# A fused chunk-selecting attention and gated FFN on one core: two more units and one more block turned by crossbar transposes, row copies issued as transfers

## The chip, the cores and the metric

The kernel runs on one core of one Trainium2 chip. The metric is device time in microseconds (us) of one launch. Where a launch was also profiled, its own time and the span that the profiler saw are given beside each other. Engines are named as in the profile: PE (matrix products, PEld its weight loads), DVE (vector), ACT (scalar), POOL (GpSimd) and SP (the engine that issues most transfers).

## What is computed

There are 4 batches of 8 heads, 768 rows and a head size of 64. Keys are cut into 24 chunks of 32 rows. For each query and chunk an upper bound of the scores is made from the chunk's smallest and largest key per dimension; the 6 chunks with the highest bound are kept, and a causal softmax attention runs over these alone. The result, 3072 rows of 512, goes through a gated FFN of width 1536.

```
k_min, k_max = min / max of each 32-row chunk of k
ub   = sum_d max(q * k_min, q * k_max);  ub[chunk after the row's own] = -1e9
sel  = the 6 chunks with the largest ub
attn = softmax(where(sel and causal, q k^T / 8, -1e9))
x    = (attn @ v) laid out as [3072, 512]
out  = (sigmoid(x @ w_gate) * (x @ w_val)) @ w_out
```

## The kernel before, in words

The 24 blocks of 128 rows (4 batches of 6) are dealt to eight units of three blocks. Unit 0 holds the first blocks of batches 0 to 2, whose rows need no selection. Unit 1 is blocks 1 to 3 of batch 0; unit 2 is blocks 4 and 5 of batch 0 and, as a third column, the first block of batch 3; unit 3 is blocks 1 to 3 of batch 1; units 4 to 7 go on through batches 1 to 3.

For each unit the work goes through the same stages. Keys are turned and reduced to chunk extremes (`keys_wide` for batch 0, `keys_blocks` for the others), and copied by rows into the key store `hk` (ops named `hk…`, line 741). Queries are turned (`turn_queries`), and `choose` makes the bounds on PE, the six largest on DVE, and mask rows, which are copied under the queries (ops `hqm…`, line 825). `attend` (line 832) does scores on PE, exponentials on ACT, the causal cut on POOL, products with the values on PE. `finish` (line 895) divides on DVE and turns the result of two heads into `xT`, so that features lie on partitions. For units 1 to 3 that turn is one PE transpose for each block (line 914), into a PSUM bank, and one copy out of it (line 918, run by the helper `copy`, lines 353 and 355); from unit 4 on (`u.i >= XBAR`, with `XBAR = 4`) it is one crossbar transfer issued by SP (line 905). `first` (line 590) does the unselected blocks: it turns keys and queries in float32 on PE (line 600), copies them out as float16 (line 604), and turns its result on PE too (line 666). Units 0 to 3 each have an FFN of their own (`ffn`: 48 gate products, 48 value products and so on, line 937, then `project_out`, line 968); units 4 and 5, and 6 and 7, share a form that needs 7 products in place of 8 (`ffn_pair`, line 1054, `project_pair`, line 1195), whose input sums (ops `S…`, line 1177) go to DVE or POOL and whose evictions (ops `E…`, `F…`) go to ACT or DVE.

What sets the order is a string, `ORDER`. It holds the 1964 operations in one list; each engine runs its own in the order of the list and waits only for the data and buffers that it needs. A word may name an engine (`hk0_u2_1@ACT`) and the buffer slots that the op takes first (`:5,2`). Without a name the first engine of the op's list is taken. The numbers in the code such as `dve(S)` or `dma=(1200, 256)` are costs that were used in making the list; they do not act at run time. SP's list is in order too: a transfer whose data is not there yet holds back those behind it.

Of the kernel before, what the change touches and what calls it, by code (L numbers as in the profile page):

```python
# [119 lines left out]
g_u0_11:1,0,11 kx1_u2_3 cm_u1_0 sc_u1_0_1:4 kt_u2_3@DVE:0 v_u0_11:7 hkf1 exp_u1_0_1 kx0_u2_3 tanh_u0_9 v16_0_3  # L120
o0_u0_0:4,0 kt_u2_0:2 hg_u0_9 tanh_u0_11 hk1_u2_3@POOL hk1_u2_0 kt_u2_1:1 sc_u1_1_1:5 q2_u2 o1_u0_0 hg_u0_11
hk0_u2_1@ACT q3_u2 kx0_u2_1 exp_u1_1_1 k11_1:0 hq1_u1_0 qf1_3:2 v16_0_2 o2_u0_0 v16_0_1 hk0_u2_3@POOL pv_u1_2:6
osb_u0_0@DVE kfT_3:3 qn_u2_3:4 sc_u1_5_0:2,2 kcr_u2 qn_u2_2:2 pv_u1_1:1 kf16_3@DVE:0 qf0_3 pv_u1_0 qT_u2_3:7 out_u0_0
rz_u1_0:0 qT_u2_2:0 sc_u1_6_2:5,3 pv_u1_3 k01_1 qf_u2_2 sc_u1_7_0:4,0 exp_u1_5_0 rz_u1_1:1 o0_u0_1:3,1 vf_3:1 qm_u2_2
qf_u2_3@DVE hq0_u2_2 x_u1_0:0 exp_u1_6_2 sc_u1_7_2:0 sc_u1_4_2:2,1 x_u1_1:2 exp_u1_7_2 sc_u1_7_1:7 o1_u0_1 exp_u1_4_2
qm_u2_3 exp_u1_7_0 qm_u2_0 sc_u1_5_2:1 hq1_u2_1 sc_u1_6_0:5 cm_u1_7 exp_u1_7_1 sc_u1_5_1:0 cm_u1_5 exp_u1_5_1
sc_u1_4_0:6 ub_u2:2,4 k10_1 exp_u1_6_0 k00_1 exp_u1_5_2 xps_u1_0:7,1 exp_u1_4_0 sc_u1_6_1:0 ubn0_u2:0 sc_u1_4_1:5
qfT_3:1 xT_u1_0 exp_u1_4_1 cm_u1_4 mx0_u2:0 o2_u0_1 hk0_u2_0@ACT hq0_u2_3@POOL ubn1_u2 exp_u1_6_1 hq1_u2_3@POOL
pv_u1_5:2 qf16_3:6 mx1_u2 cm_u1_6 pv_u1_7:6 vc_3@ACT pv_u1_4 v_0_5:5 hq1_u2_0@DVE pv_u1_6 rz_u1_2:0 scf_3:7,5,0 ap1_u2
o0_u0_2:4,0 apt1_u2:0 expf_3_0 ap0_u2 expf_3_1:2 rz_u1_3:1 x_u1_2:1 o1_u0_2 cmf_3_0 hqm1_u2_0@ACT apt0_u2 cmf_3_1  # L130
x_u1_3:0 v_0_4:3 xps_u1_1:0 hq1_u2_2 sc_u2_4_2:1,1 xps_u1_2:7 hqm0_u2_2@DVE osb_u0_1 pvf_3_0:5 xps_u1_3:2 o2_u0_2
xT_u1_1@ACT xT_u1_3 out_u0_1 xT_u1_2 hqm1_u2_2@DVE sc_u2_3_0:6,3 v_1_1:4 kx0_1_3 pvf_3_1:3 sc_u2_7_2:2,0 exp_u2_3_0
sc_u2_3_2:0 q00_1:1 g_u1_0:7,3,12 exp_u2_3_2 rzf_3_1:0 cm_u2_3 xf_3_1:2 osb_u0_2 v_u1_0:6 q01_1 hqm0_u2_0 rzf_3_0:0
xf_3_0:1 tanh_u1_0 sc_u2_3_1:0 v16_0_5 kx1_1_1:0 exp_u2_7_2 g_u1_1:3,1,13 exp_u2_3_1 v16_0_4 v_u1_1:4 kx1_1_0
exp_u2_4_2 k16_1_3:3 tanh_u1_1 xpsf_3_0:5,0 xpsf_3_1:7 sc_u2_1_1:2,2 hg_u1_1 sc_u2_1_2:0 k16_1_0:5 g_u1_2:1,2,14
exp_u2_1_2 kx1_1_3 exp_u2_1_1 pv_u2_3:3 k16_1_1:4 q10_1 sc_u2_7_1:4 xTf_3_0@ACT kx1_1_2 sc_u2_1_0:0 tanh_u1_2 v_u1_2:2
exp_u2_1_0 sc_u2_0_0:5,3 hg_u1_2 g_u1_3:1,0,15 cm_u2_1 k16_1_2:2 hg_u1_0 sc_u2_0_2:0 v_u1_3:2 v_1_3:0 tanh_u1_3
kx0_1_2 xTf_3_1@ACT g_u1_4:6,1,16 exp_u2_7_1 hg_u1_3 sc_u2_0_1:1 kt_1_0:0 tanh_u1_4 pv_u2_1:7 v_u1_4:4 exp_u2_0_0
q11_1 sc_u2_2_1:2,2 cm_u2_0 hg_u1_4 g_u1_5:6,2,17 exp_u2_2_1 kx0_1_1 sc_u2_2_0:5 exp_u2_0_1 v_u1_5:4 tanh_u1_5 kx0_1_0
sc_u2_7_0:2 exp_u2_0_2 sc_u2_4_0:1 g_u1_6:6,3,0 hg_u1_5 k11_2:0 v_u1_6:0 kt_1_1:6 tanh_u1_6 v_1_0:2 exp_u2_7_0 pv_u2_0  # L140
kt_1_3:1 sc_u2_2_2:4 g_u1_7:6,0,2 exp_u2_2_2 exp_u2_2_0 hg_u1_6 sc_u2_4_1:2 v_u1_7:4 tanh_u1_7 qf0_u3_2:0 cm_u2_2
exp_u2_4_0 g_u1_8:5,1,1 kt_1_2:3 v16_1_3 out_u0_2 pv_u2_2 hk1_u2_1@POOL k10_2 tanh_u1_8 qf0_u4_0:1 sc_u2_6_1:0,3
kcr_1@POOL sc_u2_6_0:6 rz_u2_1:0 v16_1_1 k00_2 exp_u2_6_1 v_u1_8:1 x_u2_1:0 qf0_u3_0 cm_u2_7 exp_u2_6_0 g_u1_9:5,2,4
hk1_1_1 qf0_u3_1 exp_u2_4_1 v_u1_9:3 qm_u3_0:0 cm_u2_6 sc_u2_6_2:0 qf0_u4_1 sc_u2_5_0:6,2 rz_u2_0:0 exp_u2_6_2 hg_u1_7
g_u1_10:2,3,3 tanh_u1_9 qf0_u3_3 v_u1_10:0 v_1_4:1 tanh_u1_10 hg_u1_9 qm_u3_2@POOL exp_u2_5_0 sc_u2_5_2:4
g_u1_11:5,0,5 hg_u1_10 hk1_1_0@ACT x_u2_0:1 v_u1_11:2 hg_u1_8 cm_u2_5 hq0_u3_2@ACT ub_u3:3,6 cm_u2_4 v_2_1:5
hq0_u3_0@POOL tanh_u1_11 v_1_2:3 hk1_1_3@ACT hg_u1_11 v16_1_0 o0_u1_0:0,1 ubn1_u3:0 hq1_u3_0@ACT hk0_1_1 qf0_u4_2
k01_2 xps_u2_0:7 o1_u1_0 ubn0_u3 hk0_1_0 hk0_1_3@ACT ubm1_u3 mx1_u3:0 o2_u1_0 exp_u2_5_2 ubm0_u3 ap1_u3 xT_u2_0@ACT
hq1_u3_2 o0_u1_1:1,0 osb_u1_0 qf0_u4_3 mx0_u3 sc_u2_5_1:5 out_u1_0 o1_u1_1 exp_u2_5_1 ap0_u3 hk0_1_2@ACT apt1_u3:0
q10_2:1 pv_u2_5:2 apt0_u3 pv_u2_6:6 q00_2 pv_u2_4 hqm1_u3_2@ACT hqm0_u3_0@DVE hqm0_u3_2 o2_u1_1 kx1_2_2:1 hk1_1_2  # L150
sc_u3_0_0:3,3 sc_u3_0_1:4 xps_u2_1:7 exp_u3_0_0 sc_u3_0_2:0 sc_u3_1_0:5,1 rz_u2_2:0 hqm1_u3_0 pv_u2_7 x_u2_2:2
osb_u1_1 o0_u1_2:3,1 kx1_2_1 q11_2 xT_u2_1@ACT cm_u3_0 exp_u3_0_1 sc_u3_1_1:2 exp_u3_1_0 rz_u2_3:0 kx0_2_1
sc_u3_3_0:1,0 exp_u3_0_2 sc_u3_6_1:7,2 o1_u1_2 cm_u3_1 exp_u3_1_1 x_u2_3:1 k16_2_3@ACT:5 v16_1_2 kx0_2_0 sc_u3_1_2:4
out_u1_1 k16_2_0:4 exp_u3_1_2 sc_u3_3_2:5 o2_u1_2 k16_2_1@ACT:1 kx1_2_0 xps_u2_3:0 xps_u2_2:4 xT_u2_2 xT_u2_3@ACT
q01_2 sc_u3_6_0:6 exp_u3_6_0 pv_u3_0:2 pv_u3_1 sc_u3_7_0:0,3 exp_u3_7_0 exp_u3_6_1 kt_2_3:3 kx1_2_3 kt_2_0:5 rz_u3_0:0
g_u2_0:4,0,1 tanh_u2_0 v_u2_0:6 v_3_0:3 sc_u3_2_0:7,1 g_u2_1:0,1,3 hg_u2_0 kx0_2_2 exp_u3_3_0 cm_u3_3 cm_u3_7 cm_u3_6
v_u2_1:1 exp_u3_3_2 k16_2_2:4 osb_u1_2 v_2_2:2 out_u1_2 sc_u3_3_1:5 exp_u3_3_1 g_u2_2:3,3,4 v_u2_2:6 exp_u3_2_0
cm_u3_2 sc_u3_2_1:7 exp_u3_2_1 g_u2_3:5,0,5 v_u2_3:4 g_u2_4:7,2,0 x_u3_0:2 qf0_u6_3:0 qf1_u4_2 kx0_2_3 qf1_u4_3
qf1_u4_1 tanh_u2_1 sc_u3_6_2:0 sc_u3_2_2:2 tanh_u2_3 hg_u2_3 qf1_u4_0 tanh_u2_2 hg_u2_2 hg_u2_1 v_u2_4:3 g_u2_5:4,0,2
hk0_2_3 tanh_u2_4 pv_u3_3:1 exp_u3_2_2 pv_u3_2 kt_2_1:0 rz_u3_1:0 qm_u4_0@ACT:0 v_u2_5:2 tanh_u2_5 hg_u2_5 hg_u2_4  # L160
sc_u3_5_0:4,1 exp_u3_5_0 x_u3_1:1 hq0_u4_2@ACT qf0_u6_2 sc_u3_7_1:6 exp_u3_7_1 v16_2_1 qm_u4_2@POOL v_3_4:4 k10_3:0
v_2_3:5 qf0_u6_1 k11_3 kcr_2@POOL ub_u4:7,5 ubn0_u4:0 ubm0_u4 sc_u3_4_2:1,0 exp_u3_6_2 sc_u3_4_0:3 exp_u3_4_0 hk0_2_0
sc_u3_5_2:4 exp_u3_5_2 g_u2_6:6,2,16 tanh_u2_6 xps_u3_1:7,1 xT_u3_1@ACT kt_2_2:1 v_u2_6:3 g_u2_7:6,0,17 tanh_u2_7
v_u2_7:7 g_u2_8:4,1,12 sc_u3_7_2:6 v_u2_8:0 sc_u3_5_1:2 ubn1_u4 ubm1_u4 mx1_u4:0 hq0_u4_0@POOL exp_u3_4_2 hk0_2_2@ACT
hq1_u4_0@POOL cm_u3_5 v16_2_2 hq1_u4_2@POOL v_1_5:0 v16_1_5 cm_u3_4 hg_u2_6 mx0_u4 ap0_u4 apt0_u4:0 hqm0_u4_2
qf0_u5_1:1 tanh_u2_8 g_u2_9:3,2,13 v_u2_9:4 g_u2_10:1,3,14 tanh_u2_9 hg_u2_7 hg_u2_9 exp_u3_7_2 exp_u3_5_1 sc_u3_4_1:6
hqm0_u4_0@DVE pv_u3_6:2 tanh_u2_10 hg_u2_8 v_u2_10:7 hg_u2_10 g_u2_11:4,2,15 v_u2_11:0 exp_u3_4_1 sc_u4_2_0:7,2
sc_u4_2_3:6 exp_u4_2_3 hk0_2_1 v_2_0:2 hk1_2_1 k01_3 k00_3 k16_3_0:4 kx0_3_0 k16_3_3:0 exp_u4_2_0 cm_u4_2 v16_1_4
pv_u3_5:1 xps_u3_0:3 sc_u4_2_1:5 exp_u4_2_1 tanh_u2_11 pv_u3_7 rz_u3_3:0 x_u3_3:2 o0_u2_0:6,1 sc_u4_3_2:5,3 exp_u4_3_2
pv_u3_4 sc_u4_0_2:4,1 sc_u4_0_3:2 exp_u4_0_3 sc_u4_3_0:7 exp_u4_3_0 hg_u2_11 o1_u2_0 o2_u2_0 osb_u2_0 sc_u4_1_0:7,0  # L170
sc_u4_3_1:2 v_3_2:0 sc_u4_3_3:5 exp_u4_3_3 xT_u3_0 qf0_u6_0 qf0_u5_3 ap1_u4 qf0_u5_2 rz_u3_2:0 sc_u4_2_2:3 hk1_2_3
qf0_u5_0 cm_u4_3 v16_2_0 exp_u4_1_0 cm_u4_1 o0_u2_1:0,0 o1_u2_1 kx1_3_3:1 hk1_2_0 hq0_u5_2@POOL hq1_u5_2@POOL
qm_u5_2@ACT:0 sc_u4_1_1:7 exp_u4_3_1 qm_u5_0@ACT exp_u4_0_2 x_u3_2:1 sc_u4_1_3:1 o2_u2_1 exp_u4_1_3 kx0_3_3 kt_3_0:3
apt1_u4 kx0_3_1 kt_3_3:4 hqm1_u4_0 xps_u3_3:2 osb_u2_1 q11_3:1 k16_3_1:5 q10_3 out_u2_0 xps_u3_2:5 xT_u3_2@ACT
# [1190 lines left out]
```

## Time and profile before

| | |
|---|---|
| median of 3 runs | 289.07 us (287.99 to 289.54) |
| the profiled execution's own time | 286.49 us |
| its span | 284.5 us |
| granted PE clock | 0.998 |
| busy: PE, DVE, ACT, POOL | 93%, 87%, 74%, 57% |
| moved by DMA | 34.28 MB, 120 GB/s on average |

The span runs from the first to the last instruction. A row of a view names a line of the kernel, an engine, an operation with its tiles and shapes, a count, the busy time in us and the mean of one in ns, and then the idle time ahead of it with what ended that. "SPq" is SP's queue: the time in which it was issuing a transfer.

### The profile page before, as it was taken

The page shows a single profiled execution, that of the slowest core. Times are in us where ns is not written, and L with a number is a line of the kernel's source. Part 1 is how long each engine was busy: PE and PEld are TensorE (multiplying, and loading weights), DVE is VectorE, ACT ScalarE, POOL GpSimd, SP SyncE. Part 2 cuts the span into 40 slices and gives each one's busy share as a digit, 9 for nine tenths or more (in the row PEclk, how much of TensorE's full clock was granted, in tenths as well). Part 3 has the DMA queues.
Part 4 walks back from the last instruction along what each step waited for, and adds up shares of the span by engine and source line. Part 5 has one row for each costly group of instructions (what it writes and reads, how often), then busy time and mean ns, then how long its engine had stood idle before and what let it go on. Part 6 is the DMA issues. An engine that isn't in the chain of part 4 may idle for free.

```text
span 284.5 us, 7266 instructions
## 1 busy us (share of the span) xinstructions
PE 265.6 (93%) x2668; PEld 180.9 (64%) x2668; DVE 248.8 (87%) x660; ACT 209.5 (74%) x457; POOL 162.1 (57%) x231
## 2 busy tenths in 40 slices
PE   1859999799999999999999999999899999999994
...
DMA  7999999999999999919335013030000211001005
GB/s 169 254 214 219 213 197 206 197 186 221 186 181 215 188 247 210 175 30 216 80 75 140 6 30 81 37 69 13 16 14 17 64 40 75 2 37 76 1 2 221
DMA packets 130035, 34.28 MB, mean 120 GB/s; under 512 B 118096, under 2 KB 127056, under 8 KB 130000
## 3 DMA queue, kind: packets, MB, share of 16 engines
...
q8 instruction: 21, 0.34, 0.5%
...
HBM read 30.67 MB, written 6.29 MB: 130 GB/s over the span
## 4 chain that ended last, share of the span: by engine, by line
PE 66%; DVE 11%; DMA 9%; SPq 4%; ACT 3%; POOL 3%; issue 2%; DVEq 0%; POOLq 0%; ACTq 0%
PE sc_u L848 9%; PE o_u L968 9%; PE g_u L937 8%; PE v_u L937 8%; PE pv_u L881 5%; DMA kq_u<-in_k_dram 5%; DMA v<-in_v_dram 4%; PE suo_u6u L1195 3%; PE suo_u4u L1195 2%; PE ube_u L787 2%; PE suv_u6u L1054 2%; DVE hg_u L1084 2%; PE sug_u6u L1054 2%; DVE hgp_u L1084 2%; SPq L538 2%
## 5 line engine op out<-in xcount | busy, mean ns | idle before, releaser
L859 ACT ACTIVATE att_u<-sc_u 128x512 f16<-128x512 f32 (+3 forms) x184 | 92.1, 552 | 15.9 <-PE sc_u L848 14.4
L865 POOL TENSOR_SCALAR_AFFINE_SELECT att_u<-att_u 128x384 f16<-128x384 f16 (+1 forms) x56 | 30.7, 556 | 44.3 <-ACT att_u L859 35.5
L937 PE MATMUL g_u<-xT_u,wg 128*128 128x384 f16 x192 | 39.1, 326 | 0.1
L937 PE MATMUL v_u<-xT_u,wv 128*128 128x384 f16 x192 | 39.0, 326 | 0.1
L968 PE MATMUL o_u<-wo,hg_u 128*128 128x512 f16 x144 | 35.3, 379 | 1.0 <-DMA wo<-in_moe_w_out_dram 1.0
L949 DVE SCALAR_TENSOR_TENSOR hg_u<-gate_u,v_u 128x384 f16<-128x384 f16 x48 | 25.1, 535 | 4.3 <-PE v_u L937 2.4
L881 PEld LDWEIGHTS <-att_u 128*128 128x128 f16 x640 | 24.9, 98 | 5.5 <-issue 1.5
L881 PE MATMUL pv_u<-v,att_u 128*128 128x65 f16 x640 | 27.3, 193 | 1.1 <-POOL v L564 1.0
L945 ACT ACTIVATE gate_u<-g_u 128x384 f16<-128x384 f32 x48 | 23.3, 495 | 6.7 <-PE g_u L937 6.5
L848 PE MATMUL sc_u<-hqe,hke 128*128 128x128 f16 (+2 forms) x220 | 27.8, 243 | 0.1
L848 PE MATMUL sc_u<-hqo,hko 128*128 128x128 f16 (+2 forms) x220 | 27.3, 243 | 0.1
L937 PEld LDWEIGHTS <-wg 128*128 128x128 f16 x192 | 18.1, 98 | 10.4 <-issue 0.8
L937 PEld LDWEIGHTS <-wv 128*128 128x128 f16 x192 | 18.1, 98 | 10.5 <-DMA wv<-in_moe_w_val_dram 0.4
L968 PEld LDWEIGHTS <-hg_u 128*128 128x128 f16 x144 | 13.2, 98 | 13.7 <-DVE kcr L572 1.3
L848 PEld LDWEIGHTS <-hke 128*128 128x128 f16 x220 | 17.0, 98 | 7.3 <-issue 1.0
L848 PEld LDWEIGHTS <-hko 128*128 128x128 f16 x220 | 16.8, 98 | 6.4 <-issue 0.9
L1177 POOL TENSOR_TENSOR v<-v,hg_u 128x384 f16<-128x384 f16 x6 | 6.0, 996 | 24.1 <-PE sug_u6u L1054 22.3
L564 POOL CAST v<-v 128x512 f16<-128x512 f32 x23 | 14.8, 644 | 7.0 <-DMA v<-in_v_dram 5.8
L900 DVE TENSOR_TENSOR x_u<-pv_u,rz_u 128x384 f16<-128x384 f32 (+1 forms) x28 | 14.7, 529 | 0.6
L1054 PEld LDWEIGHTS <-Sg 128*128 128x128 f16 x96 | 9.1, 98 | 6.1 <-issue 1.4
L810 DVE MAX8 mx_u<-ubn_u 128x8 f32<-128x8 f32 (+16 forms) x152 | 12.5, 158 | 0.3
L1054 PEld LDWEIGHTS <-Sv 128*128 128x128 f16 x96 | 9.0, 98 | 5.4 <-issue 0.5
(280 smaller groups left out, 699.3 us busy)
## 6 DMA issues: line engine op xcount, KB each, us to landing
...
```

The lines of the kernel that those rows point to most:

```text
L564: plan.add(f"v16_{b}_{ib}", {POOL: pool(H * D)}, lambda e: nc.gpsimd.tensor_copy(v16[b % 2][:, ib, :, 0:D], at(t)), reads=[t], writes=[("v ...
L848: nc.tensor.matmul(at(t)[:, o:o + 128 * m], hk[b % 2][e_][:, p, 128 * jb:128 * jb + 128], hq[u.side][e_][:, p, 128 * x:128 * (x + m)], sta ...
L859: plan.add(f"exp_{u.name}_{h}_{y}", {ACT: act(n)}, lambda e, t=t, att=att, b0=b0, n=n: nc.scalar.activation(at(att)[:, b0:b0 + n], at(t), ...
L865: nc.gpsimd.affine_select(out=dv, in_=dv, compare_op=ALU.is_ge, fill=0.0, base=0, pattern=[[0, u.m], [1, 128]], channel_multiplier=-1)
L881: nc.tensor.matmul(at(pv)[:, last, x, :], at(att)[:, c:c + 128], v16[b % 2][:, jb, h, :], start=(jb == 0), stop=(jb == ib))
L900: plan.add(f"x_{u.name}_{p}", {DVE: dve(u.t)}, lambda e: nc.vector.tensor_tensor(at(x_).rearrange("p a (e d) -> p e a d", e=2), at(pv)[:, ...
L937: nc.tensor.matmul(at(t), w16[:, c, 128 * fb:128 * fb + 128], at(u.xt)[:, c, :], start=(c == 0), stop=(c == 3))
L945: plan.add(f"tanh_{u.name}_{fb}", {ACT: act(T)}, lambda e, g=g, gate=gate: nc.scalar.activation(at(gate), at(g), AF.Tanh, scale=0.5), read ...
L949: plan.add(f"hg_{u.name}_{fb}", {DVE: dve(T)}, lambda e, w_=w_, gate=gate, hg=hg: nc.vector.scalar_tensor_tensor(at(hg), at(gate), 1.0, at ...
L968: nc.tensor.matmul(at(o), hgs[c][1][1]()[:, 128 * tb:128 * tb + 128], wo16[:, fc, lo:hi], start=(c == 0), stop=(c == NFB - 1))
L1054: nc.tensor.matmul(at(t), left[i](c), right[i](c), start=first and c == 0, stop=c == 1, skip_group_check=not first)
L1195: nc.tensor.matmul(at(t), sums[what[i][0], f][1]()[:, 128 * tb:128 * tb + 128], what[i][1](f), start=first and f == 0, stop=f == half - 1, ...
```

## The change

- `XBAR` goes from 4 to 2. Units 2 and 3 turn their attention output by crossbar transfers (8 of them) in place of PE transposes and copies.
- `first` for unit 2, that is the first block of batch 3, first casts keys and queries to float16 rows (two ops `kfc_3`, on ACT, and `qfc_3`, on POOL), then turns each by one crossbar transfer of 128 x 512 (`kf16_3`, `qf16_3`), and turns its result by two more (`xTf_3_0`, `xTf_3_1`).
- The helper `copy` can issue a transfer on SP. In the new list 12 of the 16 key row copies `hk…` of batches 2 and 3 are marked `@SP` (all eight of batch 3, four of batch 2), and 9 mask row copies `hqm…` of units 5 to 7.
- A chunk-extreme buffer takes a slot of the full 24 chunks (384 bytes a partition) whatever it holds.
- A flag (`port`) that the list's maker read is set otherwise for one kind of `hg` op.
- `ORDER` is written anew from its word 247 on (of 1964, now 1954): the 12 PE transpose ops leave it, two casts enter it, and many ops change their place, slots and engine. Counted by engine: DVE has 5 more of the sums `S…` and 3 more of the evictions `F…`, POOL 5 fewer `S…` and 4 more of the clamps `qm…`, ACT 5 fewer `hk…`.

```diff
-XBAR = 4
+XBAR = 2
...
     def at(b):
         if b.tile is None:
-            b.tile = pools.get(f"{b.kind}{b.slot}", pools.get(b.kind, rot)).tile(b.shape, b.dtype, tag=f"{b.kind}{b.slot}", name=b.name)
+            shape = [128, NP, NC] if b.kind == "kx" else b.shape
+            t = pools.get(f"{b.kind}{b.slot}", pools.get(b.kind, rot)).tile(shape, b.dtype, tag=f"{b.kind}{b.slot}", name=b.name)
+            b.tile = t[:, :, 0:b.shape[2]] if b.kind == "kx" else t
         return b.tile
...
+        elif e == SP:
+            nc.sync.dma_start(o, i)
...
         for n in "kq":
+            if u.i >= XBAR:
+                flat = Buf("np", f"{n}fc_{b}", [128, H * D], F16)
+                plan.add(f"{n}fc_{b}", {POOL: pool(H * D), DVE: dve(H * D, 2), ACT: act(H * D, False)}, lambda e, n=n, flat=flat: copy(
+                    e, at(flat), at(raw[n]).rearrange("s h d -> s (h d)")), reads=[(raw[n], 0), (raw[n], 1)], writes=[flat], port=True, prio=next_())
+                half[n] = Buf("np", f"{n}f16_{b}", [128, NP, 128], F16)
+                plan.add(f"{n}f16_{b}", {SP: (60, 60)}, lambda e, h=half[n], flat=flat: nc.sync.dma_start_transpose(out=at(h), in_=at(flat)),
+                         reads=[flat], writes=[half[n]], prio=next_(), dma=(1200, 256))
+                continue
...
+            if u.i >= XBAR:
+                op = plan.add(f"xTf_{b}_{e_}", {SP: (60, 60)}, lambda e, x_=x_, e_=e_: nc.sync.dma_start_transpose(
+                    out=at(u.xt)[:, 2 * e_:2 * e_ + 2, cols], in_=at(x_).rearrange("s p d -> s (p d)")),
+                    reads=[x_], writes=[(u.xt, c, x) for c in (2 * e_, 2 * e_ + 1)], prio=next_(), dma=(1200, 256))
+                plan.hold(op, u.xt) if u.xt not in op.bufs else None
+                continue
...
-                plan.add(f"hk{e_}_{b}_{p}", {POOL: pool(S), DVE: dve(S, 4, 64), ACT: act(S, False, 64)},
+                plan.add(f"hk{e_}_{b}_{p}", {POOL: pool(S), DVE: dve(S, 4, 64), ACT: act(S, False, 64), **({SP: (60, 60)} if b > 1 else {})},
...
-                plan.add(f"hqm{e_}_{u.name}_{p}", {POOL: pool(2 * u.n), DVE: dve(2 * u.n, 4, 64), ACT: act(2 * u.n, False, 64)},
+                plan.add(f"hqm{e_}_{u.name}_{p}", {POOL: pool(2 * u.n), DVE: dve(2 * u.n, 4, 64), ACT: act(2 * u.n, False, 64),
+                                                   **({SP: (60, 60)} if u.i > 3 else {})},
...
-                                 prio=next_(EV))
+                                 port=c != 2, prio=next_(EV))
```

From the new list, around the end of unit 2's attention and the start of its FFN (the places that the prediction speaks of):

```diff
+pv_u2_4 rz_u2_2:0 x_u2_2:2 k16_2_1@ACT:2 hq1_u3_2@POOL cm_u2_6 cm_u2_7 pv_u2_7:4 xT_u2_2 pv_u2_6 rz_u2_3:0 x_u2_3:0
+xT_u2_3 o1_u1_1 o2_u1_1 osb_u1_1 out_u1_1 k16_2_2:1 kt_2_2:3 kx1_2_3:1 kx1_2_2 kx0_2_2 hqm0_u3_2 sc_u3_3_1:4,2
+exp_u3_3_1 sc_u3_2_2:3,0 hqm0_u3_0 sc_u3_1_2:2,3 exp_u3_1_2 hq1_u3_0@POOL sc_u3_3_0:1 v_1_2:4 sc_u3_3_2:0
+k16_2_3@ACT:1 sc_u3_0_0:5,1 exp_u3_0_0 mx1_u3 ap1_u3 kx1_2_1 sc_u3_2_0:7 exp_u3_2_0 cm_u3_2 o0_u1_2:6,0 o1_u1_2
+v16_1_0 q10_2 kx0_2_1 kt_2_1:0 sc_u3_1_1:5 exp_u3_1_1 o2_u1_2 exp_u3_3_0 cm_u3_3 sc_u3_1_0:5 exp_u3_1_0 g_u2_0:7,3,0
```

More of the change, by code (lines that the diff above doesn't have):

```diff
@@ L120 @@
[L120 to L174, printed above, removed]
```

270 lines of the change are left out of this document (160 added, 110 removed).

## The prediction, made before the change was run

> **What bounds the kernel now.** The page comes first: how busy each engine is, and where.
>
> ```profile
> span 284.5 us, 7266 instructions
> PE 265.6 (93%) x2668; PEld 180.9 (64%) x2668; DVE 248.8 (87%) x660; ACT 209.5 (74%) x457; POOL 162.1 (57%) x231
> PE   1859999799999999999999999999899999999994
> DMA  7999999999999999919335013030000211001005
> ```
>
> PE leads, and its row of 40 slices is full but for the start, a dip at slices 11 and 12, and the end. The transfers are the other full row, up to about 125 us; after that they are nearly idle. The same by stages (columns: length, busy time of PE, PEld, DVE, ACT, POOL, clock, DMA share, GB/s):
>
> ```profile
> 0.00:60.00 60.00, 47.08 (x401) 31.75 (x401) 43.17 (x131) 37.09 (x80) 32.73 (x61) 1.00 1.07 207
> 60.00:165.00 105.00, 104.90 (x1202) 69.75 (x1200) 98.10 (x299) 85.86 (x180) 70.53 (x103) 1.00 0.82 155
> 165.00:225.00 60.00, 58.27 (x657) 39.05 (x657) 58.16 (x130) 54.18 (x119) 39.83 (x50) 1.00 0.13 32
> 225.00:260.00 35.00, 34.47 (x248) 24.22 (x248) 32.76 (x70) 21.99 (x55) 8.72 (x10) 1.00 0.13 44
> 260.00:284.50 24.50, 20.86 (x168) 16.11 (x165) 16.63 (x35) 10.39 (x26) 10.25 (x11) 0.98 0.23 87
> ```
>
> From 60 to 165 us PE idles for 0.10 us. Here only fewer or cheaper PE instructions make the kernel shorter. From 165 to 225 us PE idles for 1.73 us and DVE, at 58.16 of 60, is as full as PE: two engines take turns. The chain of work that ended last says so too:
>
> ```profile
> PE 66%; DVE 11%; DMA 9%; SPq 4%; ACT 3%; POOL 3%; issue 2%; DVEq 0%; POOLq 0%; ACTq 0%
> ```
>
> **The change part by part.** *1. PE work that goes.* Units 2 and 3 lose 4 x 2 + 4 x 3 = 20 float16 transposes, the first block of batch 3 loses 4 (its output) and 8 in float32 (keys and queries). What one costs on a full PE is read from the chain, where those that bind are listed (start, length, count):
>
> ```profile
> 52.68 0.47 PE kfT L600 x4
> 69.50 0.22 PE xpsf L666 x4
> 130.00 0.34 PE xps_u L914 x6
> ```
>
> So 57 ns and 55 ns for a float16 one, 118 ns for a float32 one: 20 x 0.057 + 4 x 0.055 + 8 x 0.118 = 2.3 us. The groups of instructions give more, because their busy time holds the drain behind the last transpose of a set:
>
> ```profile
> L914 PE MATMUL xps_u<-ident,x_u 128*128 128x128 f16 x32 | 3.4, 219 | 0.0
> L666 PE MATMUL xpsf<-ident,xf 128*128 128x128 f16 x16 | 2.4, 262 | 2.1 <-DVE xf L659 2.1
> L600 PE MATMUL kfT<-ident,kf 128*128 128x128 f32 x16 | 3.7, 389 | 0.0
> L600 PE MATMUL qfT<-ident,qf 128*128 128x128 f32 x16 | 3.9, 392 | 5.8 <-POOL hke L357 5.8
> ```
>
> By these it is 20 x 3.4/32 + 4 x 2.4/16 + 8 x 7.6/32 = 4.6 us. On a PE that never idles the drain is covered by the next product, so I take 2.3 us and keep 4.6 as the far end.
>
> *2. Work that leaves the other engines.* Ten copies out of PSUM (0.25 to 0.49 us each), two of 128x512 (0.69 and 0.59), and 21 row copies, mostly on POOL and ACT at 0.82 us, go:
>
> ```profile
> L353 ACT COPY xT_u<-xps_u 128x384 f16<-128x384 f16 x4 | 1.9, 486 | 0.0
> L355 DVE COPY xT_u<-xps_u 128x384 f16<-128x384 f16 x4 | 1.3, 343 | 0.3 <-PE xps_u L914 0.3
> L357 POOL COPY hke<-kt 64x768 f16<-64x768 f16 x6 | 4.9, 820 | 0.1
> L353 ACT COPY hke<-kt 64x768 f16<-64x768 f16 x3 | 2.5, 823 | 0.0
> L355 DVE COPY hke<-kt 64x768 f16<-64x768 f16 x3 | 1.7, 555 | 0.0
> ```
>
> The 21 alone are about 17 us at 0.82, spread over three engines. Two casts come in, at about the 0.59 to 0.69 us of the copies that they replace. Up to 165 us all this stands beside a PE that is full, so it gives nothing there except slack. From 165 to 225 us it can shorten the turns between DVE and PE. What it can give at most is PE's idle time there, 1.73 us, and at least nothing, because few of the ops that go are DVE's. I take half, 0.9 us. What is late next there is DVE itself, at 97%.
>
> *3. What DVE gets.* The new list gives DVE five more sums and three more evictions of the last products, and one more of `E`:
>
> ```profile
> L1177 DVE TENSOR_TENSOR hgp_u<-hg_u,hgp_u 128x384 f16<-128x384 f16 x4 | 2.0, 525 | 0.0
> L355 DVE COPY c0v_u4u<-suv_u4u 128x384 f32<-128x384 f32 x4 | 2.2, 551 | 0.2 <-ACT gate_u4u L1079 0.2
> L1204 DVE TENSOR_SCALAR osb_u6u<-sro_u6u 128x256 f32<-128x256 f32 x2 | 0.8, 417 | 0.2 <-PE sro_u6u L1195 0.2
> ```
>
> That is 5 x 0.525 + 0.551 + 3 x 0.417 = 4.4 us, mostly after 225 us, where DVE idles for 35 - 32.76 + 24.5 - 16.63 = 10.1 us. I cost it at nothing under that cover; without it, up to 4.4 us.
>
> *4. What the transfers cost.* 12 crossbar transfers are added to 16. Those of before:
>
> ```profile
> L905 SPq DMA_TRANSPOSE xT_u<-x_u x8: 1187/1201/2322, 140.9 to 174.7; - x8
> DMA to landing us min/median/max: 2.3/2.9/4.1
> ```
>
> Each holds SP's queue for 1.2 us (12 x 1.2 = 14.4 us of SP) and lands 2.9 us after. In their place stood some 0.2 to 0.3 us of PE and a copy of 0.25 to 0.49. So the turn of a pair becomes about 3 us later, and this is free as long as something else fills PE. For unit 2, the new list has 14 PE ops between its last transfer (`xT_u2_3`) and the first gate product that reads it (`g_u2_0`): five output groups and nine score groups of unit 3, though four or so of these wait for mask rows of their own. By the chain's rows
>
> ```profile
> 94.73 0.86 PE o_u L968 x4
> 112.41 0.55 PE sc_u L848 x6
> ```
>
> they are 5 x 0.86 + 9 x 0.55 = 9.3 us of cover. Unit 3's stretch is built alike, in a time with idle transfers. The 21 row copies are a form that the trace of before does not have: a transfer between two places in SBUF. Its nearest rows are the crossbar transfers, 2.3 to 4.1 us to landing, and the loads of values:
>
> ```profile
> L558 SPq DMA_DIRECT2D v<-in_v_dram x23: 368/835/6976, 24.0 to 186.2; - x23
> DMA to landing us min/median/max: 2.9/4.1/24.2
> ```
>
> So between 2.3 and 24.2 us; I take 3, since they are issued after 130 us where the DMA row is nearly empty. All but one have several us of PE work between issue and the scores that read them, and that one (`hk1_2_3`, next to `sc_u4_7_0` in the list) has its key tile ready long before, so SP, which runs ahead of its place, should have sent it. At nothing, then; 3 us if it does not. Behind waiting transposes stand the loads of values of batch 1 (`v_1_2`, `v_1_3`, `v_1_1`), whose casts the value products of unit 3 wait for; the gate products of unit 2 lie between. Bytes: 21 x 98 KB more on a row that is idle then. The full-width buffers and the flag cost nothing: the operations read the same number of elements.
>
> *The sum.* -2.3 (PE) - 0.9 (DVE and PE taking turns) + 0 + 0 = -3.2 us. The profiled execution took 286.49 us (span 284.5 and 2 us around it), so 283.3 us; the median of the runs shown is 289.07, 2.6 above it, which gives **285.9 us**.
>
> **Rivals.**
>
> *A. The transfers of unit 2 come late (slower).* They are issued at about 95 to 110 us, where DMA is still over 90% busy, on the one SP queue that also carries the loads; before, the first was at 140.9 us. A load there can take long. The chain of before has one that held the kernel:
>
> ```profile
> 39.32 12.24 DMA v<-in_v_dram
> ```
>
> With two issues of 1.2 us and 12.2 to landing, `g_u2_0` would wait 14.6 - 9.3 = 5.3 us, and PE has its later work queued behind it: 289.07 - 3.2 + 5.3 = 291.2 us. With 24.2 it would be 303. It ends more than 0.5% slower from a landing of about 11.6 us on, and eats the whole gain from 10.1. For it: DMA's full row, and SP's order. Against it: loads of that stretch mostly land in about 4 to 5 us.
>
> The Trainium skill (DMA: Bandwidth & Descriptors, "Queues, rings and completion order") says that each DMA engine consumes its ring in order, so a turned tile stands behind the loads that SP issued before it; no row of before shows a transpose under load. The Trainium skill (VectorE: DVE Perf Modes, "The three transpose paths" and "Rules for kernel authors") gives 390 ns for a 128x128 turn on TensorE and 1309 ns by the crossbar, and advises TensorE if PSUM will do. By that, the 32 tiles would cost an estimated 32 x 0.92 = 29 us more in latency; the trace agrees on the direction, with 57 ns on a full PE against 2.9 us to landing, but latency counts only where the cover of rival A runs out.
>
> *B. DVE gives it back at the end (about the same).* If the 4.4 us of part 3 fall on the path, the result is 285.9 + 4.4 = 290.3. For it: in the stretch from 225 to 260 us DVE is at 94%. Against it: 10.1 us of idle time to the end.
>
> *C. The relief counts in full (much faster).* 4.6 us of PE, PE's idle time from 165 to 260 us (1.73 + 0.53), and the dip between 40 and 60 us, where PE is busy 17.71 of 20:
>
> ```profile
> 40.00:60.00 20.00, 17.71 (x176) 11.09 (x175) 11.87 (x37) 15.11 (x39) 7.23 (x15) 1.00 1.05 197
> ```
>
> Together -9.2 us: 279.9. Against it: that dip is a wait for loads, and the change adds to the transfers.
>
> That the turns do not leave PE at all can be ruled out: the operations are gone from the list.
>
> **How the numbers follow.** The forecast (its own range 283.5 to 287.6) has 0.45, C and what lies below 283.5 has 0.13, B and other ways to end within 0.5% have 0.17, A and its like 0.25. About 0.5% is what a measurement of this kernel can tell from no change: 287.6 to 290.5 us. So faster 0.58, the same 0.17, slower 0.25. The range runs from 281.0, a little above C, to 291.5, a little above A at its nearest; I leave 0.06 below it and 0.13 above.
>
> **What would show it.** PE's busy time should fall by 2 to 5 us from 265.6, with no row of L914 after unit 1. Between 60 and 165 us PE should stay without idle time; an idle stretch of some us ahead of the first gate products of unit 2, released by a DMA, would be A. The landing of the new transposes should read near 3 us, not near 12. ACT should lose some 10 us and DVE about nothing. DVE at over 95% from 225 us on, with PE waiting for it in the last 50 us, would be B. The prediction is wrong if the new order opens waits that have nothing to do with the turns: over 80% of the list is rewritten, and a full PE shows each wait in the time.

## The result, and the profile after

| | before | after |
|---|---|---|
| median of 20 runs each, taken side by side | 288.12 us (285.78 to 289.54) | 291.64 us (288.61 to 294.27) |
| the profiled execution's own time, its span | 286.49, 284.5 us | 288.61, 286.6 us |

The ratio after to before is 1.0108, 95% interval 1.0083 to 1.0133: about 3 us slower. The forecast was 285.9 us, with a range of 281.0 to 291.5. The profiled execution of after is the shortest of its 20, so the traces show 2.1 of the 3.5 us between the medians. Comparisons leave disturbed runs out; the profiles of e3, e4 and e7 below are of such executions (295.6, 294.3 and 294.3 us), so I take from them which wait stands where, and times from the medians.

From the page of after: busy time, the two full rows, the chain.

```profile
span 286.6 us, 7252 instructions
PE 263.6 (92%) x2636; PEld 178.7 (62%) x2636; DVE 244.7 (85%) x656; ACT 200.6 (70%) x434; POOL 154.2 (54%) x227
...
PE   1759998999999797999999999999999979999995
...
DMA  6999999999988699998993465300021100201105
...
PE 58%; DMA 15%; DVE 12%; SPq 7%; ACT 4%; issue 3%; POOL 0%; DVEq 0%; ACTq 0%
```

PE has 2.0 us less to do, and its row now dips at slices 14 and 16 (93 to 100 and 107 to 115 us), where before it was full. DMA and SP's queue hold 22% of the chain, 13% before. The DMA row is high up to slice 21, before up to 17 and in 19. By stages:

```profile
0.00:60.00 60.00, 48.11 (x403) 32.28 (x404) 43.29 (x133) 35.51 (x75) 38.73 (x74) 0.94 1.08 204
60.00:165.00 105.00, 99.57 (x1109) 64.54 (x1108) 89.74 (x263) 76.57 (x158) 65.31 (x91) 1.00 0.91 173
165.00:225.00 60.00, 59.41 (x707) 40.77 (x703) 57.43 (x146) 56.55 (x124) 31.48 (x45) 1.00 0.25 60
225.00:260.00 35.00, 33.20 (x237) 22.96 (x238) 33.69 (x69) 20.98 (x51) 13.84 (x15) 1.00 0.13 44
260.00:286.60 26.60, 23.33 (x189) 18.16 (x187) 20.59 (x49) 10.94 (x28) 4.80 (x5) 1.00 0.19 70
```

Length less PE's busy time is its idle time. Stage by stage it goes from 12.92 to 11.89, from 0.10 to **5.43**, from 1.73 to 0.59, from 0.53 to 1.80 and from 3.64 to 3.27 us: 4.06 us more in all, less 1.95 us of work, is the span's 2.1 us. The loss stands between 60 and 165 us. What PE waited for there (sum, times, longest), then DVE and ACT:

```profile
PE v_u L956 <- DVE x_u L919: 1.9, 1, 1.9
PE sc_u L867 <- DVE x_u L919: 1.9, 1, 1.9
PE sc_u L867 <- ACT gate_u L964: 1.2, 1, 1.2
```
```profile
DVE qf_u L772 <- DMA q<-in_q_dram: 4.3, 3, 3.0
DVE x_u L919 <- DMA xT_u<-xf: 2.0, 1, 2.0
...
DVE xf L671 <- DMA xT_u<-xf: 1.6, 1, 1.6
...
DVE x_u L919 <- DMA xT_u<-x_u: 0.8, 1, 0.8
```
```profile
ACT osb_u L996 <- DMA out_dram<-osb_u: 4.8, 2, 3.3
```

Before, none of the listed waits of DVE or ACT in this stretch ended with a transfer. Now PE waits for DVE, and DVE waits in two ways. It waits to write an `x` tile, because a turn that has not yet read the tile's buffer still holds it (there are 3 such buffers): 2.0 + 1.6 + 0.8 us. And it waits for query loads: 4.3 us. ACT waits for stores to free an output tile. The order on SP's queue shows why these belong together:

```profile
88.89 1.19 SPq L924 DMA_TRANSPOSE xT_u<-x_u  x1
90.18 1.19 SPq L675 DMA_TRANSPOSE xT_u<-xf  x1
91.41 1.78 SPq L998 DMA_DIRECT2D out_dram<-osb_u  x1
93.29 1.19 SPq L924 DMA_TRANSPOSE xT_u<-x_u  x1
94.58 0.53 SPq L552 DMA_DIRECT2D q<-in_q_dram  x1
95.20 3.75 SPq L924 DMA_TRANSPOSE xT_u<-x_u  x2
...
104.07 3.53 SPq L552 DMA_DIRECT2D q<-in_q_dram  x2
```

Unit 2's turns (L924) and the block's (L675) sit between stores and loads in one queue. The two query loads at 104.07 are those that DVE then waits 3.0 us for. The DMA share in two stretches, before and after:

```profile
88.00:100.00 12.00, 12.00 (x137) 6.88 (x122) 11.00 (x42) 10.45 (x21) 8.28 (x14) 1.00 1.14 209
136.00:150.00 14.00, 14.00 (x168) 10.33 (x167) 12.47 (x39) 11.63 (x26) 9.93 (x13) 1.00 0.27 67
```
```profile
88.00:100.00 12.00, 9.84 (x96) 5.69 (x95) 8.40 (x35) 7.39 (x15) 4.22 (x8) 1.00 0.68 132
136.00:150.00 14.00, 12.83 (x113) 8.47 (x111) 11.83 (x35) 10.22 (x23) 5.35 (x10) 1.00 1.12 217
```

While the turns are issued the DMA engines move less (1.14 to 0.68), and much is moved late (0.27 to 1.12). SP issued for 7.3 of the 12 us from 88 to 100 us on five turns (the rows above: 3 x 1.19 + 3.75). Not all of this is unit 2's doing, nor is all of it costly. The same stretches in e8, which has this list without unit 2's turns and is level with before:

```profile
88.00:100.00 12.00, 11.55 (x113) 6.86 (x111) 11.04 (x42) 9.50 (x21) 4.96 (x9) 1.00 0.88 173
136.00:150.00 14.00, 12.05 (x117) 8.26 (x116) 11.37 (x34) 9.40 (x23) 5.69 (x10) 1.00 0.99 211
```

So most of the late share belongs to the new list. The same holds for SP's queue: summed over its rows from 60 to 165 us it was issuing for about 64 of the 105 us before, for 95 in after and still for 91 in e8, so a queue that is nearly full is not by itself the loss.

### The profile page after: what moved, and what is told of

It is laid out like the page before. It is cut to its first block, busy times and chain, and to the rows that moved or that the text cites. A ratio compares the mean times of both kernels' runs of the same rounds, so it can differ in the third digit from the quotient of the medians.

```text
span 286.6 us, 7252 instructions
## 1 busy us (share of the span) xinstructions
PE 263.6 (92%) x2636; PEld 178.7 (62%) x2636; DVE 244.7 (85%) x656; ACT 200.6 (70%) x434; POOL 154.2 (54%) x227
## 4 chain that ended last, share of the span: by engine, by line
PE 58%; DMA 15%; DVE 12%; SPq 7%; ACT 4%; issue 3%; POOL 0%; DVEq 0%; ACTq 0%
PE sc_u L867 9%; PE o_u L987 8%; DMA wo<-in_moe_w_out_dram 6%; PE pv_u L900 5%; DMA q<-in_q_dram 4%; PE v_u L956 4%; PE g_u L956 4%; PE suo_u6u L1214 3%; PE ube_u L805 3%; PE sug_u6u L1073 2%; PE suv_u6u L1073 2%; SPq L552 2%; PE sug_u4u L1073 2%; ACT att_u L878 2%; SPq L531 2%
## 5 line engine op out<-in xcount | busy, mean ns | idle before, releaser
L884 POOL TENSOR_SCALAR_AFFINE_SELECT att_u<-att_u 128x384 f16<-128x384 f16 (+1 forms) x56 | 29.9, 543 | 44.6 <-ACT att_u L878 33.8
L956 PE MATMUL v_u<-xT_u,wv 128*128 128x384 f16 x192 | 39.1, 326 | 1.9 <-DVE x_u L919 1.9
L956 PE MATMUL g_u<-xT_u,wg 128*128 128x384 f16 x192 | 39.1, 326 | 0.2 <-DVE hg_u L968 0.2
L867 PE MATMUL sc_u<-hqo,hko 128*128 128x128 f16 (+2 forms) x220 | 28.6, 244 | 1.5 <-ACT gate_u L964 1.2
L867 PE MATMUL sc_u<-hqe,hke 128*128 128x128 f16 (+2 forms) x220 | 26.3, 243 | 1.9 <-DVE x_u L919 1.9
L900 PE MATMUL pv_u<-v,att_u 128*128 128x65 f16 x640 | 26.4, 194 | 0.0
L956 PEld LDWEIGHTS <-wv 128*128 128x128 f16 x192 | 18.2, 98 | 13.0 <-DVE x_u L919 2.2
L956 PEld LDWEIGHTS <-wg 128*128 128x128 f16 x192 | 18.2, 97 | 11.9 <-issue 1.3
L592 POOL TENSOR_SCALAR qm_u<-qf_u 128x768 f32<-128x768 f32 (+3 forms) x11 | 17.3, 1579 | 4.1 <-DVE qf_u L772 4.0
L1196 POOL TENSOR_TENSOR v<-hgp_u 128x384 f16<-128x384 f16 x5 | 4.9, 996 | 19.9 <-DVE hgp_u L1103 17.0
L772 DVE STREAM_TRANSPOSE qf_u<-q 128x384 f32<-128x384 f32 (+2 forms) x28 | 11.4, 438 | 4.3 <-DMA q<-in_q_dram 4.3
```

The lines of the kernel that those rows point to most:

```text
L592: (nc.vector if e == DVE else nc.gpsimd).tensor_scalar_max(o, i, 0.0)
L867: nc.tensor.matmul(at(t)[:, o:o + 128 * m], hk[b % 2][e_][:, p, 128 * jb:128 * jb + 128], hq[u.side][e_][:, p, 128 * x:128 * (x + m)], sta ...
L884: nc.gpsimd.affine_select(out=dv, in_=dv, compare_op=ALU.is_ge, fill=0.0, base=0, pattern=[[0, u.m], [1, 128]], channel_multiplier=-1)
L900: nc.tensor.matmul(at(pv)[:, last, x, :], at(att)[:, c:c + 128], v16[b % 2][:, jb, h, :], start=(jb == 0), stop=(jb == ib))
L956: nc.tensor.matmul(at(t), w16[:, c, 128 * fb:128 * fb + 128], at(u.xt)[:, c, :], start=(c == 0), stop=(c == 3))
```

## The experiments

**Theory 1**: unit 2's turns make transfers late, and everything that waits for a transfer in order with them (x buffers, query loads, stores). **Theory 2**: the rewritten list makes waits, whatever turns the pairs. **Theory 3**: the row copies on SP do it. Lines in the experiments have numbers some lower than in after (L952 for L956), as their lists are wrapped otherwise. All ratios are to the kernel before, run beside on the same chip (its medians were 286.1 to 288.3 us).

| run | what | ratio, 95% interval |
|---|---|---|
| after | the change | 1.0108, 1.0083 to 1.0133 |
| e6 | units 2 and 3 turned on PE again | 1.0019, 0.9984 to 1.0053 |
| e8 | unit 2 alone turned on PE again | 0.9989, 0.9959 to 1.0019 |
| e3, e7 | single waits mended | 1.0086, 1.0054 to 1.0118; 1.0089, 1.0050 to 1.0128 |
| k3, k5 | before, with turns of units 2 and 3; of unit 3 alone | 1.0217, 1.0177 to 1.0258; 1.0077, 1.0039 to 1.0115 |
| e5, e9 | row copies back on POOL; on their old engines | 1.0619, 1.0576 to 1.0662; 1.0560, 1.0520 to 1.0601 |
| k4 | before, with row copies on SP | 1.0131, 1.0096 to 1.0166 |
| e10 | unit 2's turns on ACT's queue | 1.0262, 1.0228 to 1.0296 |
| e12, e14 | seven stores off SP; left out | 1.0118, 1.0063 to 1.0173; 0.9949, 0.9923 to 0.9974 |
| e4 | four sums back on POOL | 1.0105, 1.0068 to 1.0142 |
| e11, again as e11b | e8 with SP's order mended | 0.9982, 0.9960 to 1.0004; 0.9989, 0.9958 to 1.0021 |
| e13, again as e13b | e11 with one sum moved | 0.9898, 0.9859 to 0.9937; 0.9935, 0.9911 to 0.9960 |

### The turns undone: e6, e8

In e6 the condition in `finish` becomes `u.i >= 4`, with these words in the list (unit 3's alike); e8 has `u.i >= 3` and unit 2's words alone.

```diff
-        if u.i >= XBAR:
+        if u.i >= 4:
...
-xT_u2_1 xT_u2_0 xT_u2_2 xT_u2_3
+sc_u2_4_2:5 xps_u2_1:6 xT_u2_1@ACT
+sc_u2_4_1:7 xps_u2_0:5 xT_u2_0@ACT
+pv_u2_6 xps_u2_2:0 xT_u2_2@ACT
+o2_u1_1 xps_u2_3:2 xT_u2_3@ACT
```

> The changed list with one part undone: the eight pair turns of units 2 and 3 go back to TensorE with a copy out of PSUM by ScalarE; batch 3's first block and the row copies stay as changed. Theory 1 (the turns' transfers make waits: x buffers held until the transfer has read them, query loads pushed back in SP's queue, VectorE waits in order, PE waits for VectorE): PE's idle time from 60 to 165 us falls from 5.4 us to under 2 us, PE gets 20 x 0.057 = 1.1 us of work back, so about 2.5 us faster than the changed kernel, level with the kernel before (288 to 289). Theory 2 (the rewritten list makes the waits, whatever turns the pairs): the idle time stays near 5 us and the time rises by 1.1 us, to about 292.

> The changed kernel with the turns of unit 2 alone back on TensorE, unit 3's stay transfers. Theory 1: the two waits of 1.85 us at 94 and 113 us go, the wait for ScalarE at 144 us (behind unit 3's turns in SP's queue) stays with 1.2 to 2.3 us; about half to two thirds of what e6 gained: 289.3 to 290.3 us. Theory 2': the clock or unit 3's turns alone carry the loss: above 290.8.

e6 took 288.8 us and e8 287.9. Their stretch from 60 to 165 us, e6 and then e8:

```profile
60.00:165.00 105.00, 103.54 (x1150) 67.42 (x1148) 91.70 (x271) 81.03 (x171) 67.54 (x93) 1.00 0.88 169
```
```profile
60.00:165.00 105.00, 101.95 (x1137) 66.44 (x1136) 92.03 (x277) 79.26 (x167) 67.33 (x94) 1.00 0.91 173
```

PE idles for 1.46 us in e6 (5.43 in after). Theory 2 falls for this loss: the same list with PE turns is level with before. e8 gained all of it, not the half to two thirds that I expected: its two waits of 1.85 us are gone, a wait for ACT of 2.0 us is left, and the 12 turns of PE work for unit 3 are saved. So **unit 2's four turns carry the loss** (1.0108 against 0.9989, some 3.4 us); unit 3's cost nothing in this list (the intervals of e6 and e8 overlap).

### Single waits mended: e3, e7

```diff
-xf_3_1:2
+xf_3_1:0
-x_u2_0:0
+x_u2_0:2
-x_u2_2:2
+x_u2_2:1
...
-qf1_u4_2
...
-qf1_u4_3 qf1_u4_1 qf0_u5_3:1
...
-qf1_u4_0 x_u3_1:0
+x_u3_1:0 qf1_u4_2 qf1_u4_3 qf1_u4_1 qf0_u5_3:1 qf1_u4_0
```

e7 adds the store's place:

```diff
+out_u2_0
 q01_3:1 q10_3
...
-o0_u2_2:4,1
+o0_u2_2:4,0
```

> The changed kernel with all its transfers, and two small edits: three x tiles get a buffer that no pending transfer holds, and VectorE's five query transposes that wait for batch 2's query loads stand behind the next normalisation (x_u3_1). Theory 1: the two PE waits of 1.85 us (at 94 and at 113 us) go, PE's idle time from 60 to 165 us falls from 5.4 to about 1.7 us, and the time by some 3.5 us, to 287.5, slightly under the kernel before. Theory 2 (waits belong to the list at large, others take their place): idle time stays above 4 us and the time within 1 us of the changed kernel.

> The kernel of e3 (changed list, x buffers and VectorE's order mended) with one more edit: the store out_u2_0 goes ahead of batch 3's query loads on SP's queue, and output block o_u2_2 takes the buffer that it frees. In e3 ScalarE waited 2.6 us for a store that SP had queued behind three turns of unit 3 and three query loads, TensorE then waited 2.3 us, and its granted clock fell to 0.75 and 0.91 in the next two stretches of 5 us, about 1.7 us more. Theory 1 (what stands behind the turns in SP's one queue makes the waits): that wait and the dip go, e3's 291.1 falls by 2 to 4 us, to 287 to 289. Theory 2 (the list makes waits at large): another wait takes its place and the time stays above 290.3.

Both missed: 291.1 and 291.3 us, within noise of after. In e3 the two waits are gone, but this stands further on (timelines of ACT and PE, then three stretches, with the granted clock third from the right):

```profile
146.10 0.60 ACT L992 ACTIVATE osb_u<-o_u 128x512 f32<-128x512 f32 x1 [2.63 <-DMA out_dram<-osb_u]
```
```profile
147.13 0.38 PE L863 MATMUL sc_u<-hqo,hko 128*128 128x128 f16 x4 [2.33 <-ACT gate_u L960]
...
149.34 1.49 PE L952 MATMUL v_u<-xT_u,wv 128*128 128x384 f16 x4
...
151.42 0.81 PE L952 MATMUL v_u<-xT_u,wv 128*128 128x384 f16 x4
```
```profile
140.00:145.00 5.00, 4.80 (x55) 3.33 (x54) 5.00 (x20) 3.06 (x7) 1.53 (x3) 1.00 1.18 198
145.00:150.00 5.00, 2.87 (x17) 1.74 (x17) 2.01 (x6) 2.97 (x7) 1.01 (x2) 0.75 1.07 233
150.00:155.00 5.00, 5.00 (x33) 3.11 (x32) 4.05 (x8) 2.89 (x9) 2.18 (x4) 0.91 0.92 205
```

ACT waits for a store that SP had behind three turns and three query loads, PE for ACT, and then PE's clock is down. In e7 that wait is gone; the last of the query loads went out at 143.13 us (140.65 in after), and DVE stood still for 4.8 us until 148.58 ahead of its query transposes (the trace names no releaser; the load would land about then). Mending one place moved the wait to the next in the queue.

### The turns alone, in the old list: k3, k5

```diff
 x_u2_1:0
+xT_u2_1
...
-xps_u2_1:7
...
-xT_u2_1@ACT
```

k3 does this for the eight pairs of units 2 and 3, k5 for unit 3's alone. Unit 2's turns stand right behind the normalisation, unit 3's at the places of the PE turns.

> The kernel before with one part of the change alone: the pair turns of units 2 and 3 by crossbar transfers, unit 2's issued right behind the normalisation, in the old list. TensorE loses 20 x 0.057 = 1.1 us. Theory 1: the turns cost more than that by their place in SP's queue: the last turn of unit 2 has some 3 us of TensorE work ahead of the gate products, and x buffers are held longer, so 1 to 4 us slower than before, 289 to 292. Theory 2 (the turns are harmless, the list of the changed kernel is at fault): 1 us faster than before, or equal.

> The kernel before with the turns of unit 3 alone by crossbar transfers, at the old places of its TensorE turns; they are issued behind most loads. With those of units 2 and 3 it was 2.2% slower. If the price lies in unit 2's stretch, where SP's queue and the DMA engines are full, these turns cost nothing: ratio 0.995 to 1.003. If a crossbar turn costs wherever TensorE is full: ratio 1.008 or more.

Both slower: 2.2% and 0.8%. PE's longest wait in k3, and two of DVE's in k5:

```profile
PE g_u L933 <- DMA xT_u<-x_u: 2.9, 1, 2.9
```
```profile
DVE kcr L568 <- DMA k<-in_k_dram: 2.5, 1, 2.5
...
DVE qf_u L750 <- DMA q<-in_q_dram: 2.0, 2, 1.5
```

k3's row is my rival A in its own place: with little cover, the gate products wait for the turn. k5 misses its expectation, and teaches more: no reader of a turned tile waits. SP's rows show its first turn at 113.48 us, among the loads, and the two key loads behind it at 117.64 us, at 113.96 before. Of these 3.7 us, 2.3 stood there already at the key load ahead of the turn (111.20 us, 108.88 before); the rest comes with the turn. So a turn seems to cost by its place in the queue as well, but how much of k5's loss that is, these rows do not settle. Why unit 3's are free in the new list was not tested.

### The row copies: e5, e9, k4

```diff
-hk0_2_1@SP
+hk0_2_1@POOL
```

e5 does this for all 21; e9 gives each its engine of before; k4 marks the same 21 `@SP` in the old list.

> The changed kernel with all 21 row copies that run as transfers put back on GpSimd, at the same places in the list. Theory 3 (the row copies as transfers cost time, by SP's queue or by landing late): 1 us or more faster than the changed kernel. Theory 1: they are beside the point, within 0.7 us of the changed kernel either way, or slower, as GpSimd gets some 17 us of work back.

> The changed kernel with its 21 row copies put back on the engines that did them before (15 GpSimd, 4 VectorE, 2 ScalarE), turns unchanged. In e5, with all 21 on GpSimd, the time rose by 14 us. If the row copies as transfers are a real relief in this list, the time rises by 3 us or more over the changed kernel, to 294 or more, with TensorE's new idle time between 125 and 225 us. If e5 only showed an overloaded GpSimd, the time stays within 1 us of the changed kernel.

> The kernel before with the 21 row copies alone as transfers on SP's queue, at their old places in the list. e9 showed that the changed list is 13 us slower without them. If they are a relief in any list: 1 to 2 us faster than before. If the changed list is merely built around them, and the old list hides the copies: within 1 us of before (287 to 289); slower only where a copy lands late for the scores that read it.

305.5, 304.8 and 290.6 us. Theory 3 falls: taken back, the copies cost 4.5 to 5.1% more. But they are no relief by themselves either. PE's waits in e9 and in k4, between 125 and 225 us:

```profile
PE pv_u L896 <- POOL att_u L880: 7.3, 4, 4.9
PE sc_u L863 <- POOL hko L357: 2.5, 1, 2.5
```
```profile
PE sc_u L864 <- DMA hko<-kt: 3.1, 1, 3.1
```

In the new list POOL's order has no room for them; in the old list a copy holds PE for 3.1 us. It was not slow (2.2 us from issue to landing); SP issued it only at 142.55 us, behind a store, a load and a turn.

### Queue or load: e10, e12, e14

e10 issues unit 2's turns from ACT, e12 seven stores; e14 leaves those stores out, so these output rows are not written.

```diff
-            op = plan.add(f"xT_{u.name}_{p}", {SP: (60, 60)}, lambda e: nc.sync.dma_start_transpose(
+            op = plan.add(f"xT_{u.name}_{p}", {ACT if u.i == 2 else SP: (60, 60)}, lambda e: (nc.scalar if u.i == 2 else nc.sync).dma_start_transpose(
```

> The changed kernel with unit 2's four turns still crossbar transfers, but issued from ScalarE's DMA queue in place of SP's (some places later in the list, where e6 and e8 had the copies out of PSUM). The DMA engines have the same work; SP's queue, which in the changed kernel was issuing for all of the 70 us from 80 to 150 us, loses some 6 us of issue time. If SP's one queue is what makes everything late: the waits for query loads and stores shrink as in e8, and the time comes to 288 to 289.5 us, with ScalarE some 6 us busier with issues. If it is the load on the DMA engines, or the x buffers held until a transfer has read them: 290.5 us or more.

> The changed kernel with all its turns as they are, but seven output stores (the last of unit 0, all of units 1 and 2) issued from ScalarE's DMA queue right behind the copy that they store. The transfers and their bytes are the same, and so are the x buffers; only SP's queue loses some 10 us of issue time between 80 and 150 us. If SP's one queue is short because of unit 2's turns: the query loads come earlier, PE's idle time from 60 to 165 us falls from 5.4 to under 3 us, and the time falls by 1 to 3 us, to a ratio of 1.000 to 1.007 to before. If it is the DMA engines' load or the x buffers: the waits for the transfers stay, the ratio stays at 1.010 or rises, as ScalarE pays for the issues.

> The changed kernel, all turns as they are, with the seven output stores of e12 left out altogether (those output rows are not written): SP issues nothing for them and the DMA engines move 1.8 MB less, 9.4 us of their work at the 190 GB/s of that stretch. e12, which moved only their issue, left the time as it was. If the load on the DMA engines sets when the query loads land: they come several us earlier, TensorE's idle time from 60 to 165 us falls under 2.5 us, the time falls to a ratio to before of 0.995 to 1.004. If the x buffers alone hold VectorE: only the wait for a store (1.2 us at 144 us) goes, ratio 1.004 to 1.008.

e10 is no test of its question. ACT's turn was issued at 85.73 us and took 2.43 us to land; SP's, next in its queue since 81.8 us, went out only at 88.23 (chain, then SP's wait):

```profile
85.73 2.43 DMA xT_u<-x_u
88.23 2.27 DMA xT_u<-xf
90.60 0.43 DVE xf L667
91.08 0.74 PE ubo_u L801
```
```profile
SPq L671 <- DMA xT_u<-x_u: 9.6, 2, 6.4
```

Here turns on two queues go one after the other, so SP's queue stood still, with its key loads; DVE then PE (4.7 us) waited. The Trainium skill (DMA: Bandwidth & Descriptors, "Silent corruption: two transposing streams in flight at once") says that software must keep transposes of two queues apart; by that, the two turns could not overlap. The trace agrees, with 88.23 right after 85.73 + 2.43. That SP's turn stood still from 81.8 to 85.73 us too, while no other was under way, is the order of this program, which has ACT's turn first.

e12 gained nothing (1.0118): the two late query loads went out at 103.19 us, 0.9 earlier than in after, though two stores of together 2.3 us (91.41 and 99.05 in after) had left the queue ahead of them, and DVE's wait for query loads stayed:

```profile
DVE qf_u L769 <- DMA q<-in_q_dram: 4.9, 3, 2.7
```

In e14 they went out at 101.04 us, PE idles for 1.33 us from 60 to 165 us, and these are DVE's waits for query loads and PE's for DVE:

```profile
DVE qf_u L769 <- DMA q<-in_q_dram: 0.6, 2, 0.4
```
```profile
PE sc_u L864 <- DVE x_u L916: 1.0, 1, 1.0
PE g_u L953 <- DVE hg_u L965: 0.3, 1, 0.3
```

1.8 MB less to move, all turns in place, and the time is 1.6% under after. The kernel before had nothing to win there without these stores, as its PE idles for 0.10 us in that stretch. So the loss is one of transfers coming late, not of the turns' latency: taking issues off SP alone is not enough, taking bytes and issues away is. Of PE's waits for an x tile, 3.7 us in after, 1.0 is left. How the rest divides between SP's issue and the pace of the DMA engines stays open.

### The end, and a version that beats both: e4, e11, e13

```diff
-S1_u4u5_3
+S1_u4u5_3@POOL
...
-S3_u4u5_0
+S3_u4u5_0@POOL
...
-S2_u4u5_4
+S2_u4u5_4@POOL
...
-S4_u4u5_4
+S4_u4u5_4@POOL
```

That is e4. e11 is e8 with `out_u2_0` ahead of `q01_3`, `o0_u2_2:4,0`, and `q11_3` ahead of `out_u2_1`. e13 is e11 with `S3_u4u5_0` (on DVE) moved behind `S4_u4u5_4`.

> The changed kernel with four sums S of units 4 and 5 back on GpSimd. If VectorE's extra work near the end holds PE (my rival B): the waits of 0.63 and 0.68 us between 229 and 234 us go, and the time falls by 0.5 to 1.3 us, to 290 to 290.7. If not: within 0.5 us of the changed kernel, or slower where GpSimd hands the sums over late.

> The kernel of e8 (unit 2 turned on TensorE) with two places on SP's queue mended: the store out_u2_0 ahead of batch 3's query loads, with o_u2_2 in the buffer that it frees, and the last of these loads ahead of the store out_u2_1. In e8 TensorE still waited 2.0 us for ScalarE, which waited 2.3 us for a store. If SP has room again without unit 2's turns, that wait goes and nothing takes its place: 285.5 to 287 us, 0.5 to 0.9% faster than before. If SP's queue is still short there, another wait of 1 to 2 us takes its place, as in e7: 287.5 to 288.5.

> The kernel of e11 (changed list, unit 2 turned on TensorE, two stores and a load at other places on SP's queue) with VectorE's sum S3_u4u5_0 moved some places later, behind the work that TensorE waits for near 229 us. If VectorE's added sums hold TensorE there (part 3 of the prediction, rival B): another 0.3 to 0.6 us, a ratio to before of 0.994 to 0.998. If not, as e11: 0.998.

> The kernel of e11 once more, beside e13's on one chip, since their ratios to before came from two chips (0.9982 and 0.9898). Its profile has the waits of 0.6 to 0.7 us near 229 us. Expected ratio 0.994 to 0.998.

> The kernel of e13 once more, beside e11's on one chip. If the moved sum counts: 0.3 to 0.6 us (0.1 to 0.2%) under e11b; its profiles show one wait of 0.3 us less, so a difference of 0.8% as between the two chips would not be the sum's. Expected ratio 0.990 to 0.997, clear of 1: a version that beats both kernels.

e4 gained nothing. e11's wait for ACT went, but its ratio, 0.9982 and 0.9989, is not clear of 1. e13 is clear of it twice, 0.9898 and 0.9935: 0.6 to 1.0% faster than before, and by the second 1.7% faster than after (286.3 and 284.9 us). PE's waits after 225 us in e11b:

```profile
PE sug_u6u L1069 <- DVE osb_u L1222: 0.7, 1, 0.7
PE sro_u4u L1210 <- DVE hqo L1192: 0.6, 1, 0.6
PE suo_u4u L1210 <- DVE hqo L1192: 0.3, 1, 0.3
```

In e13b the first two stand as they are and the third is gone, so the moved sum accounts for 0.3 us. On one chip the two differ by 0.5%, with intervals that just touch; what more than 0.3 us there is, stays open.

## Why the prediction was wrong, step by step

*Part 1* (PE work, -2.3 us) was right: PE's busy time fell by 2.0, although part of the first 60 us ran at a lower clock (0.94, 1.00 before) and took 1.0 us more.

*Part 2* (turns of DVE and PE from 165 to 225 us, -0.9) came out near: PE's idle time there fell by 1.14. It is not the row copies alone: with these (k4) it is 1.58 us, 1.73 before. ACT lost 8.9 us of work, some 10 forecast; DVE lost 4.1, about nothing forecast.

*Part 3* (DVE's 4.4 us at nothing) was mis-sized: between 225 and 260 us PE's idle time rose by 1.27 us, with waits of 0.7 and 0.6 us for DVE. Of rival B's 4.4 us that is about a third. Of the 10.1 us of DVE idle time that I set against it, 24.5 - 16.63 = 7.9 lay after 260 us, behind the place where PE needs the sums. e4 shows that POOL does them no better: with four sums there the two waits are 1.4 and 1.0 us.

*Part 4* (transfers at nothing) **is the step that failed**. Its landing time held: 2.3/2.6/5.2 us for the pairs' turns (2.3/2.9/4.1 before), and 2.0/2.3/4.6 for the row copies; `g_u2_0` waited for no turn, and no score for a row copy. Its hold on SP's queue did not: the 12 added turns held it for some 22 us, 14.4 forecast, one of them for 3.96. The main fault was to ask only who reads a turned tile. Not asked was who waits for the buffer that the turn reads: 4.4 us of DVE waits. And of what stands behind in SP's queue I named three value loads, for which PE did not wait, and not the query loads `q00_2` and `q11_2` (DVE, 4.3 us) and the stores (ACT, 4.8 us). PE, with no slack from 60 to 165 us, passed on 5.4 us of it.

*Rival A* had the cause (one SP queue, DMA over 90% busy, unit 2) and the sign, 291.2 us, near the 291.64 measured, but the wrong place: not the gate products but DVE's next tiles. That its number is so near is luck: its wait of 5.3 us never came there, and it started from the median of three runs, 289.07 us, where the 20 gave 288.12. In k3, without cover, it came true where I had put it. Its chance of 0.25 was too low, since I tied it to that one place and one price.

The sentence that the transfers were the other full row up to 125 us stood at the head of the prediction, and part 4 did not use it: what is put on a full row comes out as lateness of whatever is behind. That paragraph also misread PE's row: it dips at slices 3 and 8 (14 to 21 and 50 to 57 us), not at 11 and 12; the forecast does not use it.
